# Squares of q and k taken by ACT ahead of the mixers, with two buffers, and two pairs' scalings on POOL

## The chip, the cores and the metric

The kernel runs on one core of one Trainium2 chip. The metric is the device time of one execution in microseconds (us); the time of a kernel is the median of its runs.

## The reference

Four batches of twelve heads (448 tokens, 64 columns) go through attention with normalised queries and keys, and its output through two mixers of tokens and channels.

```python
def rmsnorm(x, g):
    return x / np.sqrt(np.mean(x * x, axis=-1, keepdims=True) + 1e-06) * g
scores = (rmsnorm(q, g_q) @ rmsnorm(k, g_k).T) / 8          # per head
attn = exp(scores - max) / (sum + 1e-9); out = attn @ v
x = out of all heads, as [4, 448, 768]
u = x + (x.T @ U @ V).T;  x = u + relu(u @ w_ch1) @ w_ch2    # first mixer, 3072 wide
u = x + (relu(x.T @ w_tok1) @ w_tok2).T
x = u + relu(u @ w_ch1') @ w_ch2'                            # second mixer, 1536 wide
```

The change touches `mean(x * x)` and the scaling of q and k by its root.

## The kernel before

All arithmetic is in 32 bits; products are made of parts (high and low) of 32-bit operands. Heads are taken in pairs: 24 pairs, numbered 0 to 23 in the order in which they are loaded (`turn`). Tokens lie on 112 partitions, four rows each.

The program has a lone stage, in which only the attention of the first two batches runs (pairs 0 to 11); a seam, in which the first mixer's weights begin to come in and the rank mix of these batches is made (`rank_mix`, x.T @ U @ V); a mixed stage, in which the first mixer of the first two batches runs with the attention of the last two among it (pairs 12 to 23); and then the mixers that are left. The generator `attention` (L505) prepares pairs ahead of the heads that it weighs, so pairs 12 to 16 are partly prepared within the lone stage.

One pair takes these steps. `fetch_heads` (L352) loads q, k and v from SP's queue; q and k share five buffers. `load_pair` (L364) squares q and k (L373, tile sq, one buffer), sums the squares per token on DVE (L374, tile ms), takes 1/sqrt by Ln and Exp on ACT (L378, L379, tile rs) and one Newton step in four small operations (L381 to L384, tile nt), and scales q and k (L392, tiles qn and kn). `split` (L143) then cuts v into a high part on ACT and a low part on POOL (tile vs). The squares and the scalings are on DVE for pairs 0, 2 and 3 and on POOL for all others; the small operations are on DVE for pair 0 and on POOL else. `turn_pair` (L404) transposes qn and kn on PE (tt), takes the high part on ACT (L417, L421) and the low part on DVE (both, one buffer for q and one for k), and copies them by DMA into qs and ks (L434, L433; L438 for pair 0), three buffers each. `softmax` (L442): two score products per quarter of a head on PE (sc, three PSUM buffers), their maximum on DVE (L451, nm), the exponential on ACT (L453, p), and the normalisation on POOL (L460). `weigh` (L463): transposition of p on PE (pt), copies into ph and pl, and the product with v.

Each engine takes its instructions in the order of its queue and waits at the head of it. The code's order is not the queues' order: a scheduler, which runs when the program is built, orders each engine's instructions by durations that it assumes, except where `keep_in_program_order` is set (the loads of the first weights). A changed instruction in the lone stage so moves others far behind it. A pool's tile that is used again makes its writer wait for the readers of the tile before.

Of the kernel before, what the change touches and what calls it, by code (L numbers as in the profile page):

```python
# [9 lines left out]
F32 = mybir.dt.float32  # L10
# [3 lines left out]
AF = mybir.ActivationFunctionType  # L14
# [10 lines left out]
def attention_then_two_mixers(  # L25
# [30 lines left out]
    nc = tc.nc  # L56
# [3 lines left out]
    CP, NC4 = 112, 4  # L60
    NP = H // 2
# [36 lines left out]
        return x.rearrange("r (p c) -> r c p", c=NC4)  # L98

    pools = {"late": False, "split_u": nc.gpsimd}  # L100
    AT = dict(qr=5, kr=5, vr=3, qn=1, vs=2, p=8, ph=3, pl=3, sq=1)

    def open_pools(stack, side):
        for nm, bufs, space in side:
            pools[nm] = stack.enter_context(tc.tile_pool(
                name=nm, bufs=bufs, **({"space": PSUM} if space else {}), reuse_waits="tile"))
# [36 lines left out]
    def split(w, hi, lo):  # L143
        nc.scalar.activation(hi, w, AF.Copy)  # L144
        nc.gpsimd.tensor_sub(lo, w, f(hi))  # L145
# [206 lines left out]
    def fetch_heads(b, hp, names):  # L352

        h0 = 2 * hp
        res = []
        for nm in names:
            t = pools["at"].tile([CP, 2, NC4, D], F32, tag="vr" if nm == "v" else "qkr", bufs=AT[nm + "r"],
                        name=f"{nm}r")
            nc.sync.dma_start(t, dict(q=q, k=k, v=v)[nm][b, h0:h0 + 2].rearrange(
                "h (p c) d -> p h c d", c=NC4))  # L360
            res.append(t)
        return res

    def load_pair(b, hp, whole, turn, qk):  # L364
        first = turn == 0
        mul = nc.vector.tensor_mul if turn in (0, 2, 3) else nc.gpsimd.tensor_mul
        qr, kr, vr = qk + fetch_heads(b, hp, "v")

        ms = pools["at"].tile([CP, 2, 8], F32, tag="ms", name="ms")
        for i, t in enumerate((qr, kr)):  # L370
            sq = pools["at"].tile([CP, 2 * NC4, D], F32, tag="sq", bufs=AT["sq"], name="sq")
            tt = t.rearrange("p h c d -> p (h c) d")
            mul(sq, tt, tt)  # L373
            nc.vector.reduce_sum(ms[:, i], sq, axis=AX.X)  # L374
        small = nc.vector if first else nc.gpsimd
        small.tensor_scalar(ms, ms, 1.0 / D, 1e-6, op0=ALU.mult, op1=ALU.add)
        rs = pools["at"].tile([CP, 2, 8], F32, tag="rs", name="rs")
        nc.scalar.activation(rs, ms, AF.Ln)  # L378
        nc.scalar.activation(rs, rs, AF.Exp, scale=-0.5)  # L379
        nt = pools["at"].tile([CP, 2, 8], F32, tag="nt", name="nt")  # L380
        small.tensor_mul(nt, rs, rs)  # L381
        small.tensor_mul(nt, nt, ms)
        small.tensor_scalar(nt, nt, -0.5, 1.5, op0=ALU.mult, op1=ALU.add)
        small.tensor_mul(rs, rs, nt)  # L384

        def scale(i, shape):
            return rs[:, i].rearrange("p (h c) -> p h c", h=2).unsqueeze(3).to_broadcast(shape)

        qn, kn = [], []
        for i, (nm, t, n) in enumerate((("qn", qr, qn), ("kn", kr, kn))):  # L390
            n.append(pools["at"].tile([CP, NC4, 2, D], F32, tag=nm, bufs=AT["qn"], name=nm))
            mul(  # L392
                n[0].rearrange("p c h d -> p h c d"), t, scale(i, [CP, 2, NC4, D]))
        qn, kn = qn[0], kn[0]

        vs = pools["at"].tile([CP, 2, NC4, 2, D], F32R, tag="vs", bufs=AT["vs"], name="vs")
        js = [j for j in range(2) if j not in whole]
        if js:
            js = slice(js[0], js[-1] + 1)
            split(vr[:, js], vs[:, js, :, 0], vs[:, js, :, 1])  # L400
        flat = vr.rearrange("p h c d -> p (h c d)")
        return qn, kn, [flat[:, j * NC4 * D:] if j in whole else vs[:, j] for j in range(2)]
# [39 lines left out]
    def softmax(pr, qs, ks, kt):  # L442
        for c in range(NC4):
# [7 lines left out]
            nc.vector.tensor_reduce(nm, sc, axis=AX.X, op=ALU.max, negate=True)  # L451
            p = pools["pp"].tile([CP, S], F32, tag="p", bufs=AT["p"], name="p")
            nc.scalar.activation(p, sc, AF.Exp, bias=nm, accum_out=sm[:, c % 2:c % 2 + 1])  # L453
# [9 lines left out]
    def weigh(pr, vj, j, dst, whole):  # L463
# [3 lines left out]
        def product(kc, ph, pl):  # L467
            if whole:
                mm(pv, vj[:, kc * D:kc * D + P], ph, kc == 0, kc == NC4 - 1)
                return  # L470
            vk = vj[:, kc].rearrange("p t d -> p (t d)")
            mm(pv, vk, ph, kc == 0, False)
            mm(pv, vk, pl, False, kc == NC4 - 1)

        last = None
        for kc in range(NC4):
# [6 lines left out]
            if last:  # L483
                product(*last)
            ph = pools["pp"].tile([CP, S], F32 if whole else F32R, tag="ph", bufs=AT["ph"],
                                  name="ph")
# [551 lines left out]
    with ExitStack() as stack:  # L1038
# [24 lines left out]
        w1s = [w1_chunk("a", wa1, j) for j in range(G)]  # L1063
        pools["late"] = False
        inner.close()
        AT.update(p=8, ph=3, pl=3)
        open_pools(stack, (("pp", 1, 0), ("g", 2 * G + 1, 0), ("p", 2, 1), ("v", 1, 1),
                           ("s", 2, 1), ("t", 1, 1), ("m", 2, 1)))
        pools["new_xs"] = lambda: pools["g"].tile([P, 2, S], F32R, tag="g", name="xs")
# [97 lines left out]
```

## Time and profile before

| | |
|---|---|
| median of three runs | 1530.44 us (1529.71 to 1535.4) |
| profiled execution | 1532.7 us, of which its span 1530.9 us |
| PE busy | 1440.5 us, 94% |
| DVE busy | 1170.5 us, 76% |
| POOL busy | 921.8 us, 60% |
| ACT busy | 742.7 us, 49% |

The page's shares are means over stages. Of its 40 slices of 38 us the first five are the lone stage; PE is busy 4, 8, 8, 9 and 9 tenths there, POOL 5, 8, 9, 9 and 8, and the granted clock of PE is at nine tenths or more in all of them; the sixth slice, the seam, has the lowest clock, 7 tenths. A busy PE isn't a PE at its peak, since a matmul's latency counts as busy.

### The profile page before, as it was taken

To read this page: it belongs to the slowest core of one execution; us is meant where nothing else is said; L and a number is where in the kernel's file an instruction comes from. 1 tells how busy PE (TensorE), PEld (TensorE's weight loads), DVE (VectorE), ACT (ScalarE), POOL (GpSimd) and SP (SyncE) were. 2 spreads that over 40 slices of the span, in tenths; PEclk is the share of its full clock that TensorE was granted. 3 is DMA by queue.
4 is the path that set the end of the run, shared out by engine and by line. 5 is a ranking of instruction groups with operands and counts; after the bars stand their busy time and mean duration, and the time that the engine had idled before them with its cause. 6 is when DMAs were issued, how large, how long until landed. Compare 5 with 4: busy or idle time off the path is not lost.

```text
span 1530.9 us, 22094 instructions
## 1 busy us (share of the span) xinstructions
PE 1440.5 (94%) x7396; PEld 1271.6 (83%) x7396; DVE 1170.5 (76%) x1793; ACT 742.7 (49%) x1508; POOL 921.8 (60%) x955
## 2 busy tenths in 40 slices
PE   4889978999999999999999999998999999999998
PEld 3667656888899889988888998897999998988997
DVE  7888777887877778666757766477888888578876
ACT  4777655656665665444535343335343431334421
POOL 5899857877876655455645454037777755206841
PEclk9999979999999999999999999999999999999999
DMA  6666545867766664765637664354545453424343
GB/s 171 159 163 162 145 162 183 250 193 218 253 220 203 184 208 171 258 227 175 214 128 240 227 231 143 116 194 134 177 127 183 127 186 129 134 85 127 119 122 103
DMA packets 144385, 266.06 MB, mean 174 GB/s; under 512 B 12832, under 2 KB 104448, under 8 KB 144160
## 3 DMA queue, kind: packets, MB, share of 16 engines
q1 hardware_dynamic: 143952, 264.65, 55.5%
q8 instruction: 59, 0.97, 0.3%
q14 instruction: 54, 0.44, 0.1%
q10 hardware_dynamic: 320, 0.00, 0.0%
HBM read 149.72 MB, written 79.10 MB: 149 GB/s over the span
## 4 chain that ended last, share of the span: by engine, by line
PE 63%; DVE 11%; POOL 8%; DMA 7%; ACT 5%; issue 4%; SPq 1%; ACTq 0%; POOLq 0%; DVEq 0%
PE ps_x L79 26%; PE ps_g L79 12%; PE ps_p L79 10%; PE pv L79 3%; PE sc L79 3%; PE pt L479 2%; POOL w_bits L134 2%; PE ps_u L79 2%; POOL w L145 2%; PE ps_t L79 2%; DMA qs<-both 2%; DVE w_bits L126 1%; POOL p L460 1%; DMA w_raw<-in_moe_w_ch_dram 1%; DMA c_a<-w_bits 1%
## 5 line engine op out<-in xcount | busy, mean ns | idle before, releaser
L79 PE MATMUL ps_x<-gs,w 128*128 128x448 f32 x1440 | 323.9, 371 | 9.6 <-DVE xT L668 5.3
L79 PE MATMUL ps_g<-u,w 128*128 128x448 f32 x1440 | 313.1, 370 | 4.3 <-DMA w<-h_a 1.8
L79 PEld LDWEIGHTS ps_x<-gs,w 128*128 128x128 f32 x1440 | 266.7, 189 | 35.4 <-DVE xT L668 8.4
L79 PEld LDWEIGHTS ps_g<-u,w 128*128 128x128 f32 x1440 | 269.4, 189 | 28.8 <-DVE u L565 2.1
L79 PE MATMUL ps_x<-gs,w_b 128*128 128x448 f32 x1026 | 228.8, 369 | 7.1 <-DVE xT L833 2.4
L79 PEld LDWEIGHTS ps_x<-gs,w_b 128*128 128x128 f32 x1026 | 192.9, 189 | 25.9 <-DVE xT L833 3.8
L134 POOL TENSOR_TENSOR w_bits<-w_bits,w_round 128x768 uint32<-128x768 uint32 (+3 forms) x80 | 144.9, 1812 | 109.3 <-DVE w_bits L131 59.5
L145 POOL TENSOR_TENSOR w<-w_bits,w 128x768 fp32r<-128x768 f32 (+3 forms) x82 | 145.4, 1780 | 73.1 <-ACT w L144 69.3
L668 DVE TENSOR_TENSOR xT<-ps_x,xT 128x448 f32<-128x448 f32 x216 | 132.2, 617 | 36.5 <-PE ps_x L79 33.7
L145 POOL TENSOR_TENSOR w_b<-w_f,w_b 128x384 fp32r<-128x384 f32 x104 | 118.3, 1152 | 59.1 <-ACT w_b L144 58.9
L295 POOL TENSOR_TENSOR w_f<-w_f 128x384 f32<-128x384 f32 x26 | 36.2, 1391 | 179.8 <-DMA w_f<-c_b 75.0
L460 POOL TENSOR_SCALAR p<-p,sm 112x448 f32<-112x448 f32 x192 | 133.1, 706 | 17.5 <-DVE sm L457 10.9
L453 ACT ACTIVATE p<-sc,nm 112x448 f32<-112x448 f32 x192 | 121.3, 635 | 45.8 <-DVE nm L451 40.3
L79 PE MATMUL sc<-ks,qs 128*112 128x448 f32 x384 | 120.9, 407 | 15.9 <-ACT p L453 11.3
L451 DVE TENSOR_REDUCE nm<-sc 112x1 f32<-112x448 f32 x192 | 116.2, 614 | 17.6 <-PE sc L79 16.8
L479 PEld LDWEIGHTS pt<-ident,p 112*112 112x112 f32 x768 | 89.8, 134 | 33.2 <-issue 10.4
L126 DVE TENSOR_SCALAR w_bits<-w_bits 128x768 f32<-128x768 f32 (+3 forms) x80 | 71.9, 898 | 56.6 <-ACT w_bits L125 56.5
L479 PE MATMUL pt<-ident,p 112*112 112x112 f32 x768 | 111.9, 261 | 2.5 <-DVE pl L494 0.8
L130 ACT ACTIVATE w_round<-w_raw 128x768 uint32<-128x768 uint32 (+3 forms) x80 | 69.8, 873 | 77.6 <-POOL w_bits L134 69.9
L490 ACT ACTIVATE ph<-pt 112x448 fp32r<-112x448 f32 (+1 forms) x168 | 88.2, 544 | 26.2 <-PE pt L479 25.5
L637 ACT ACTIVATE gs<-ps_g 128x448 fp32r<-128x448 f32 x88 | 47.3, 541 | 108.8 <-PE ps_g L79 107.9
L125 ACT ACTIVATE w_bits<-w_raw 128x768 f32<-128x768 f32 (+3 forms) x80 | 69.8, 874 | 61.7 <-POOL w L145 33.1
(141 smaller groups left out, 2766.2 us busy)
## 6 DMA issues: line engine op xcount, KB each, us to landing
w_raw<-in_moe_w_ch_dram SPq DMA_DIRECT2D x72, 768.0 KB, 5.1
w_b<-h_a SPq DMA_DIRECT2D x65, 384.0 KB, 4.3
h_a<-w SPq DMA_DIRECT2D x56, 384.0 KB, 3.1
ks<-both SPq DMA_DIRECT2D x92, 224.0 KB, 3.8
c_a<-w_bits SPq DMA_DIRECT2D x40, 384.0 KB, 4.7
w_f<-c_a SPq DMA_DIRECT2D x40, 384.0 KB, 3.2
h_b<-w SPq DMA_DIRECT2D x32, 384.0 KB, 2.6
w_b<-h_b SPq DMA_DIRECT2D x29, 384.0 KB, 3.8
```

Source lines behind the costliest of these rows:

```text
L79: nc.tensor.matmul(o, lhsT=l, rhs=r, start=start, stop=stop)
L125: nc.scalar.activation(f(w), f(high), AF.Abs)
L126: nc.vector.tensor_scalar_max(f(w), f(w), TINY)
L130: nc.scalar.activation(r, low, AF.Copy, scale=2.0 ** -29)
L134: nc.gpsimd.tensor_tensor(w, w, r, op=ALU.add)
L145: nc.gpsimd.tensor_sub(lo, w, f(hi))
L451: nc.vector.tensor_reduce(nm, sc, axis=AX.X, op=ALU.max, negate=True)
L453: nc.scalar.activation(p, sc, AF.Exp, bias=nm, accum_out=sm[:, c % 2:c % 2 + 1])
L460: nc.gpsimd.tensor_scalar(x, x, sm[:, i:i + 1], 1.0, op0=ALU.mult, op1=ALU.mult)
L479: nc.tensor.transpose(pt[:, c * CP:(c + 1) * CP], pr[c][:, kc * CP:(kc + 1) * CP], ident[:CP, :CP],)
L490: nc.scalar.activation(ph, pt, AF.Copy)
L668: nc.vector.tensor_add(xT[:, dc], px, xT[:, dc])
```

## The change

Pair 0's q and both q and k of pairs 1 to 11 are squared by ACT (`AF.Square`); pair 0's k stays on DVE; from pair 12 on the squares stay on POOL. The scalings of pairs 2 and 3 go from DVE to POOL. The squares get two buffers; ms and nt get one instead of two; pl has two instead of three in the mixed stage.

```diff
--- before.py
+++ after.py
@@ -98,7 +98,7 @@
         return x.rearrange("r (p c) -> r c p", c=NC4)
 
     pools = {"late": False, "split_u": nc.gpsimd}
-    AT = dict(qr=5, kr=5, vr=3, qn=1, vs=2, p=8, ph=3, pl=3, sq=1)
+    AT = dict(qr=5, kr=5, vr=3, qn=1, vs=2, p=8, ph=3, pl=3, sq=2)
 
     def open_pools(stack, side):
         for nm, bufs, space in side:
@@ -363,21 +363,26 @@
 
     def load_pair(b, hp, whole, turn, qk):
         first = turn == 0
-        mul = nc.vector.tensor_mul if turn in (0, 2, 3) else nc.gpsimd.tensor_mul
+        mul = nc.vector.tensor_mul if first else nc.gpsimd.tensor_mul
         qr, kr, vr = qk + fetch_heads(b, hp, "v")
 
-        ms = pools["at"].tile([CP, 2, 8], F32, tag="ms", name="ms")
+        ms = pools["at"].tile([CP, 2, 8], F32, tag="ms", bufs=1, name="ms")
         for i, t in enumerate((qr, kr)):
             sq = pools["at"].tile([CP, 2 * NC4, D], F32, tag="sq", bufs=AT["sq"], name="sq")
             tt = t.rearrange("p h c d -> p (h c) d")
-            mul(sq, tt, tt)
+            if turn >= NP * 2:
+                nc.gpsimd.tensor_mul(sq, tt, tt)
+            elif first and i:
+                nc.vector.tensor_mul(sq, tt, tt)
+            else:
+                nc.scalar.activation(sq, tt, AF.Square)
             nc.vector.reduce_sum(ms[:, i], sq, axis=AX.X)
         small = nc.vector if first else nc.gpsimd
         small.tensor_scalar(ms, ms, 1.0 / D, 1e-6, op0=ALU.mult, op1=ALU.add)
         rs = pools["at"].tile([CP, 2, 8], F32, tag="rs", name="rs")
         nc.scalar.activation(rs, ms, AF.Ln)
         nc.scalar.activation(rs, rs, AF.Exp, scale=-0.5)
-        nt = pools["at"].tile([CP, 2, 8], F32, tag="nt", name="nt")
+        nt = pools["at"].tile([CP, 2, 8], F32, tag="nt", bufs=1, name="nt")
         small.tensor_mul(nt, rs, rs)
         small.tensor_mul(nt, nt, ms)
         small.tensor_scalar(nt, nt, -0.5, 1.5, op0=ALU.mult, op1=ALU.add)
@@ -1063,7 +1068,7 @@
         w1s = [w1_chunk("a", wa1, j) for j in range(G)]
         pools["late"] = False
         inner.close()
-        AT.update(p=8, ph=3, pl=3)
+        AT.update(p=8, ph=3, pl=2)
         open_pools(stack, (("pp", 1, 0), ("g", 2 * G + 1, 0), ("p", 2, 1), ("v", 1, 1),
                            ("s", 2, 1), ("t", 1, 1), ("m", 2, 1)))
         pools["new_xs"] = lambda: pools["g"].tile([P, 2, S], F32R, tag="g", name="xs")
```

Lines behind the edit have numbers higher by five (L378 to L383, L392 to L397, L453 to L458). Three places, one of them on two engines, show how the queues' orders move. Numbers behind a tile's name count the tiles in the order of the code; qr_113, kr_115 and vr_121 are loads of pair 0, qr_117, kr_119 and vr_182 of pair 1, qr_178 and kr_180 of pair 2.

The head of the program on ACT: rs_131 is pair 0's root, both_151 and both_159 are its turned q and k. Before:

```order
L378 ACTIVATE rs_131<-ms_123 112x16
L379 ACTIVATE rs_131<-rs_131 112x16
L144 ACTIVATE vs_143<-vr_121 112x4x64
L144 ACTIVATE vs_204<-vr_182 112x4x64
L417 ACTIVATE both_151<-tt_146,gg_78 128x448
L421 ACTIVATE both_159<-tt_154 128x448
L378 ACTIVATE rs_192<-ms_184 112x16
L379 ACTIVATE rs_192<-rs_192 112x16
```

Now, from the second square on:

```order
L378 ACTIVATE sq_185<-qr_117 112x512
L144 ACTIVATE vs_143<-vr_121 112x4x64
L378 ACTIVATE sq_188<-kr_119 112x512
L383 ACTIVATE rs_131<-ms_123 112x16
L144 ACTIVATE vs_204<-vr_182 112x4x64
L384 ACTIVATE rs_131<-rs_131 112x16
L378 ACTIVATE sq_280<-qr_178 112x512
L383 ACTIVATE rs_192<-ms_184 112x16
L384 ACTIVATE rs_192<-rs_192 112x16
L422 ACTIVATE both_151<-tt_146,gg_78 128x448
L378 ACTIVATE sq_283<-kr_180 112x512
L426 ACTIVATE both_159<-tt_154 128x448
```

The two operations of rs_131 stood first; now two squares and the two splits of v stand ahead of or between them, and the square of kr_180 stands ahead of both_159.

POOL in the lone stage, while pair 0 and pair 1 are normalised (L460, L465) and pairs 3 and 4 are prepared (rs_502 and nt_505 are pair 3's, sq_710 and sq_713 pair 4's). Before:

```order
L381 TENSOR_TENSOR nt_505<-rs_502 112x16
L456 TENSOR_SCALAR sm_337<-sm_337 112x2
L373 TENSOR_TENSOR sq_710<-qr_488 112x512
L382 TENSOR_TENSOR nt_505<-nt_505,ms_494 112x16
L456 TENSOR_SCALAR sm_374<-sm_374 112x2
L460 TENSOR_SCALAR p_343<-p_343,sm_337 112x448
L460 TENSOR_SCALAR p_358<-p_358,sm_337 112x448
L383 TENSOR_SCALAR nt_505<-nt_505 112x16
L456 TENSOR_SCALAR sm_414<-sm_414 112x2
L373 TENSOR_TENSOR sq_713<-kr_490 112x512
L460 TENSOR_SCALAR p_380<-p_380,sm_374 112x448
L460 TENSOR_SCALAR p_397<-p_397,sm_374 112x448
```

Now:

```order
L465 TENSOR_SCALAR p_343<-p_343,sm_337 112x448
L465 TENSOR_SCALAR p_358<-p_358,sm_337 112x448
L386 TENSOR_TENSOR nt_505<-rs_502 112x16
L387 TENSOR_TENSOR nt_505<-nt_505,ms_494 112x16
L461 TENSOR_SCALAR sm_374<-sm_374 112x2
L388 TENSOR_SCALAR nt_505<-nt_505 112x16
L389 TENSOR_TENSOR rs_502<-rs_502,nt_505 112x16
L397 TENSOR_TENSOR qn_510<-qr_273,rs_502 112x2x4x64
L397 TENSOR_TENSOR kn_512<-kr_275,rs_502 112x2x4x64
L381 TENSOR_SCALAR ms_709<-ms_709 112x16
L465 TENSOR_SCALAR p_380<-p_380,sm_374 112x448
L465 TENSOR_SCALAR p_397<-p_397,sm_374 112x448
```

The squares of pair 4 are gone from between the normalisations; the scalings of pair 3 (qn_510, kn_512) have come, and the sums of pair 4 (ms_709) are taken up right behind them.

ACT at the same place, among the exponentials (p). Before:

```order
L453 ACTIVATE p_358,sm_337<-sc_353,nm_356 112x448
L417 ACTIVATE both_465<-tt_460,gg_78 128x448
L453 ACTIVATE p_380,sm_374<-sc_375,nm_378 112x448
L453 ACTIVATE p_397,sm_374<-sc_392,nm_395 112x448
L490 ACTIVATE ph_316<-pt_311 112x448
L453 ACTIVATE p_420,sm_414<-sc_415,nm_418 112x448
L421 ACTIVATE both_473<-tt_468 128x448
L453 ACTIVATE p_438,sm_414<-sc_433,nm_436 112x448
L490 ACTIVATE ph_351<-pt_345 112x448
L453 ACTIVATE p_523,sm_517<-sc_518,nm_521 112x448
```

Now:

```order
L458 ACTIVATE p_380,sm_374<-sc_375,nm_378 112x448
L383 ACTIVATE rs_502<-ms_494 112x16
L378 ACTIVATE sq_710<-qr_488 112x512
L384 ACTIVATE rs_502<-rs_502 112x16
L378 ACTIVATE sq_713<-kr_490 112x512
L458 ACTIVATE p_397,sm_374<-sc_392,nm_395 112x448
L458 ACTIVATE p_420,sm_414<-sc_415,nm_418 112x448
L378 ACTIVATE sq_925<-qr_703 112x512
L495 ACTIVATE ph_388<-pt_383 112x448
L495 ACTIVATE ph_410<-pt_403 112x448
L458 ACTIVATE p_438,sm_414<-sc_433,nm_436 112x448
```

Three squares of pairs 4 and 5 stand among the exponentials and the copies of the transposed p (ph).

ACT in the seam: xs are parts of the transposed x, u the mixed x, w_bits and w_round the first steps of a weight chunk. Before:

```order
L586 ACTIVATE xs<-ps_h 128x384
L558 ACTIVATE xs<-pt_x 112x384 x2
L564 ACTIVATE u<-xT 128x448
L558 ACTIVATE xs<-pt_x 112x384
L564 ACTIVATE u<-xT 128x448
L558 ACTIVATE xs<-pt_x 112x384
L125 ACTIVATE w_bits<-w_raw 128x768
L130 ACTIVATE w_round<-w_raw 128x768
L564 ACTIVATE u<-xT 128x448
L125 ACTIVATE w_bits<-w_raw 128x768
```

Now:

```order
L591 ACTIVATE xs<-ps_h 128x384
L563 ACTIVATE xs<-pt_x 112x384 x2
L569 ACTIVATE u<-xT 128x448
L125 ACTIVATE w_bits<-w_raw 128x768
L130 ACTIVATE w_round<-w_raw 128x768
L569 ACTIVATE u<-xT 128x448
L563 ACTIVATE xs<-pt_x 112x384 x2
L125 ACTIVATE w_bits<-w_raw 128x768
L569 ACTIVATE u<-xT 128x448
L144 ACTIVATE w<-w_bits 128x768
```

The second chunk's w_bits and w_round have moved ahead of the second u and of the last turned parts of x.

## Rows read from the trace of the kernel before

**Rows 1.** Stretches: us, busy of PE, PEld, DVE, ACT, POOL; clock, DMA, GB/s
```profile
22.00:60.00 38.00, 32.23 (x159) 23.54 (x160) 32.29 (x67) 26.51 (x74) 28.97 (x57) 0.91 0.70 176
60.00:100.00 40.00, 34.72 (x203) 25.68 (x201) 33.91 (x72) 29.15 (x82) 33.68 (x60) 1.00 0.66 159
100.00:130.00 30.00, 28.54 (x162) 20.72 (x161) 25.04 (x53) 23.74 (x67) 27.58 (x52) 1.00 0.61 150
130.00:196.00 66.00, 61.13 (x347) 43.64 (x345) 54.82 (x114) 46.63 (x127) 58.14 (x112) 1.00 0.64 159
196.00:245.00 49.00, 36.26 (x150) 28.56 (x150) 35.85 (x48) 27.42 (x50) 31.29 (x22) 0.79 0.45 154
245.00:560.00 315.00, 302.23 (x1638) 267.77 (x1639) 256.39 (x441) 196.41 (x410) 228.84 (x251) 0.99 0.71 219
```

**Rows 2.** Chain of work by line, 22 to 130 us, then 130 to 165
```profile
by line: PE sc L79 15.8%; PE pv L79 14.9%; DMA qs<-both 11.9%; PE pt L479 9.4%; DMA ks<-both 8.9%; issue 8.3%; ACT p L453 7.1%; SPq L433 5.3%; PE tt L410 3.8%; ACT ph L490 3.4%; DVE nm L451 2.2%; SPq L434 2.0%; ACT w L144 1.2%; ACT both L41
...
by line: POOL p L460 14.3%; issue 12.8%; DMA qs<-both 10.3%; DMA kr<-in_k_dram 8.8%; DVE nm L451 6.5%; POOL sq L373 6.0%; PE pv L79 4.5%; DVE both L418 3.7%; DVE ms L374 3.6%; DVE ph L488 3.3%; PE sc L79 3.1%; POOL qn L392 3.0%; POOL sm L45
```

**Rows 3.** Weight loads of PE waiting, 22 to 130: us, times, longest
```profile
PEld sc L79 <- ACT p L453: 10.1, 16, 1.7
```

**Rows 4.** Groups, 22 to 130: busy, mean ns of one, idle before it
```profile
L453 ACT ACTIVATE p<-sc,nm 112x448 f32<-112x448 f32 x64 | 40.4, 637 | 6.0 <-DVE nm L451 3.9 <-PE pt L479 2.0
...
L373 POOL TENSOR_TENSOR sq<-qr 112x512 f32<-112x512 f32 x8 | 8.6, 1080 | 2.2 <-DMA qr<-in_q_dram 1.7
...
L373 POOL TENSOR_TENSOR sq<-kr 112x512 f32<-112x512 f32 x8 | 8.3, 1039 | 0.5 <-DMA kr<-in_k_dram 0.3
...
L392 POOL TENSOR_TENSOR qn<-qr,rs 112x512 f32<-112x512 f32 x6 | 6.3, 1043 | 0.4
```

**Rows 5.** The same view, whole execution, one shape on ACT
```profile
L144 ACT ACTIVATE vs<-vr 112x512 fp32r<-112x512 f32 x12 | 7.5, 627 | 2.7 <-PE pv L79 2.7
```

**Rows 6.** The head in order of time: start, us, instruction, idle before it
```profile
0.72 1.28 ACT L82 ACT_TABLE_LOAD   x1 [0.72 <-PEq L1151]
...
7.93 0.17 DVE L381 TENSOR_TENSOR nt<-rs 112x16 f32<-112x16 f32 x1
...
8.41 0.42 ACT L144 ACTIVATE vs<-vr 112x256 fp32r<-112x256 f32 x1 [1.58 <-DMA vr<-in_v_dram]
...
9.69 1.48 DVE L392 TENSOR_TENSOR qn<-qr,rs 112x512 f32<-112x512 f32 x1
...
9.80 0.42 ACT L144 ACTIVATE vs<-vr 112x256 fp32r<-112x256 f32 x1 [0.97 <-DMA vr<-in_v_dram]
...
11.20 0.31 SPq L359 DMA_DIRECT2D kr<-in_k_dram  x1
...
13.41 0.54 ACT L421 ACTIVATE both<-tt 128x448 fp32r<-128x448 f32 x1 [0.44 <-PE tt L410]
...
14.91 2.48 SPq L438 DMA_DIRECT2D ks<-both  x4
...
18.00 1.43 PE L79 MATMUL sc<-ks,qs 128*112 128x448 f32 x3
...
20.60 0.69 DVE L392 TENSOR_TENSOR qn<-qr,rs 112x512 f32<-112x512 f32 x1 [2.09 <-POOL rs L384]
...
21.82 0.62 DVE L451 TENSOR_REDUCE nm<-sc 112x1 f32<-112x448 f32 x1
```

**Rows 7.** DMA issues up to 14 us: KB each, us to landing
```profile
kr<-in_k_dram SPq DMA_DIRECT2D x3, 224.0 KB, 3.4
```

**Rows 8.** The start of the rank mix in order of time
```profile
206.34 11.43 SPq L116 DMA_DIRECT2D w_raw<-in_moe_w_ch_dram  x3
...
213.09 0.91 ACT L125 ACTIVATE w_bits<-w_raw 128x768 f32<-128x768 f32 x1
```

**Rows 9.** DMA issues, whole execution: KB each, us to landing
```profile
w_raw<-in_moe_w_ch_dram SPq DMA_DIRECT2D x72, 768.0 KB, 5.1
```

**Rows 10.** Writes of pl, 245 to 570 us: ns min, median, max
```profile
L494 DVE TENSOR_TENSOR pl<-pt,ph x80: 593/615/626, 264.2 to 567.0; 112x448 fp32r<-112x448 f32 x80
```

## The prediction

> **What bounds the kernel now.** I read the stretches first [rows 1], since the shares of a whole span mix stages with different limits. From 245 to 560 us PE is busy 302.2 of 315 us, so what ACT and POOL do there matters only where PE is idle; behind that stretch the queues' orders are the same with and without the change. From 196 to 245 us, the seam with the first weights, PE has 36.3 of 49 us at a mean granted clock of 0.79. The attention alone ("lone stage") runs up to 196 us, and there no engine has the whole time: between 22 and 130 us PE is busy 32.2 + 34.7 + 28.5 = 95.5 of 108 us (12.5 idle), DVE 91.2, POOL 90.2, ACT 79.4. The edited squares lie almost all in this part: sixteen on POOL between 22 and 130 us [rows 4]. After 130 us POOL squares only for pair 12 and later (pair 11's second square is the last ahead of it), and those stay with POOL.
>
> Second, the chain of work that ended last [rows 2]. Between 22 and 130 us it runs through PE (score, transposition and value products, 43.9% together with tt), through the copies of the turned q and k (qs and ks, 20.8%) and through ACT's exponentials (7.1%). No POOL line is among those named there. Between 130 and 165 us POOL does carry it: its normalisations have 14.3%, its squares 6.0%. The reader is to see that the busy engine and the engine on the chain are not the same before 130 us, and that where POOL's squares are on the chain, they are the ones that the change leaves alone.
>
> Third, what PE waits for between 22 and 130 us [rows 3]: 10.1 us in 16 waits for ACT to have read a score tile. ACT is the idlest of the four by busy time and yet the one that PE waits for, because its queue is in order.
>
> **The change part by part.** I work against the profiled execution, 1532.7 us with a span of 1530.9, and carry the differences over to the median of the three runs, 1530.4.
>
> *The head.* Before, the first correction of pair 0 (nt) starts at 7.93 and the scaled q at 9.69 [rows 6]. Now Ln of pair 0 stands on ACT behind the split of v (vr_121) and behind the square of kr_119, and the split of the next v stands between Ln and Exp. Those splits start at 8.41 and 9.80, each the moment its load landed [rows 6]; nothing moves these loads. So: split 8.41 to 8.83, square (0.63) to 9.46, Ln to 9.67, next split 9.80 to 10.22, Exp to 10.43, against nt at 7.93 before: 2.5 us later. DVE has one more reduction of this shape ahead of rs, so rs is some 3 us late; the scaled q, which took 1.48 us beside POOL's work, should now take the 0.69 of the same operation at 20.60 [rows 6], and starts near 12.7. The sixth q or k load (kr_180) waits for that q's buffer: before it was issued at 11.20, as the scaling at 9.69 ended; now near 13.4 and lands 3.4 us later [rows 7], at 16.8. On ACT the square of kr_180 now stands ahead of pair 0's turned k (both_159), which before began at 13.41 [rows 6]; it is held until 17.4. From the issue of the ks copies to the first scores it was 14.91 to 18.00, 3.1 us; so now 18.0 to 21.1 [rows 6]. That is 3.1 us late, but before, the first maximum did not follow the scores: it waited until 21.82, because DVE stood in front of the scaling of pair 2 (20.60, idle 2.09 for POOL) [rows 6]. That scaling is on POOL now, and the maximum can follow its second score products by about 1.9 us, near 23.0. The head costs **+1.2**; the bounds are -0.5 (if loads and copies land earlier than I shift them) and +3.1 (the scores' whole delay).
>
> *DVE loses five squares and four scalings.* Those before 21.8 us are in the head. Behind it lie one square and the two scalings of pair 3, 3 x 0.69 = 2.0 us [rows 6], on an engine that is busy 32.3 of 38 us [rows 1]. PE is idle 5.8 us in that stretch, partly for copies that no DVE square holds up. I take half: **-1.0**, bounds 0 and -2.0.
>
> *POOL loses sixteen squares* between 22 and 130 us, 8.6 + 8.3 = 16.9 us, and gets two scalings at 1.04 [rows 4], net 14.8 us of 90.2. This is the change's main effect and is off the chain [rows 2]. It can only help through what queues behind a square: the normalisations that PE's transpositions need. The ceiling is PE's idle time of 6.7 us from 60 to 130 us [rows 1] and a little before, 7. Since no POOL line is on that chain I take less than half: **-3.0**, bounds 0 and -7.
>
> *ACT gets the squares*: 23 of them (pair 0's q, both of pairs 1 to 11). The nearest row is the split of v in the same shape, 112x512, 0.627 us [rows 5]; the other end is the exponential, 0.637 for 448 columns [rows 4], 0.73 for 512. I take 0.63: 14.5 us. Six of them fall before 22 us; the other 17, 10.7 us, raise ACT's busy time up to 130 us from 79.4 to 90.1 us, 13%. If what PE waits for ACT grows in proportion, 10.1 x 0.13 = **+1.3**; bounds 0 (the squares fall into ACT's idle time, 28.6 us) and +5 (half of those 10.1 us again).
>
> The Trainium skill's page "ScalarE: Activation LUTs", section "Rules for kernel authors", speaks against this move: multiplications belong on VectorE, not on ScalarE. The rows show 0.63 for ACT's pass over this shape and 0.69 for DVE's multiplication of it [rows 5, 6]; by the page's rule the 17 squares would lie on DVE as 11.7 us beside its 91.2, which would fill 95% of the 108 us. Here the measurement decides against the rule: per square ACT is not slower.
>
> *Seam.* ACT now reaches the second weight chunk (w_bits, w_round) ahead of u and of the last turned x. Its load goes out at 206.34 [rows 8] and takes about 5.1 us [rows 9], so it lands near 211.5; before, ACT took it at 213.09 [rows 8]. Now u and x come up to two instructions of 0.91 later, but the chunk is ready 1.5 us sooner. **+0.5**, bounds 0 and +2.
>
> *What costs nothing.* pl with two buffers: of 80 writes [rows 10] I set each against the reads of PE, and only one came while two earlier ones were unread; it would wait for one read, on DVE, with PE busy. ms and nt with one buffer: the next pair's sums now wait until nt has been multiplied by ms; the order puts the sums behind that multiplication, so I price it at 0; if a sum does stand in front of it, the maxima queue behind it on DVE (in ACT's +5). sq with two buffers lets POOL square q and k in a row in the mixed stage, beside a full PE: 0. The orders of the mixed stage differ up to about 560 us; its 12.8 us of PE idle time [rows 1] can move by some 3 us either way, with no sign.
>
> Sum: +1.2 - 1.0 - 3.0 + 1.3 + 0.5 = -1.0: 1531.7 against the profiled 1532.7, and **1529.5** from the median of 1530.4.
>
> **The rivals.** *Relief pays in full.* POOL's shorter queue brings normalisations and scaled q and k forward, and the copies of qs and ks, a fifth of the chain, start earlier. Then the two gains reach their ends, -2 - 7, ACT's cost and the seam are 0 and the head +0.5: 1522; with 3 us from the mixed stage 1519. For it: POOL is busy 27.6 of 30 us at 100 to 130 us. Against: POOL is not on the chain there. *ACT's queue is blocked*, slower than before. A square stands at the head of ACT's queue until its load has landed; on POOL one such wait of 1.7 us is on the rows [rows 4], where only POOL paid. On ACT the exponentials and the turned q and k queue behind it, and PE waits for these. Pairs 3 to 11 have 17 squares behind 22 us; if half of them wait 1 us each, that is +8.5, and with the head at +3.1 and the other gains halved about +10: 1540. It decides from about one wait of 1 us in every pair on. *The change doesn't do what it says*: if Square needed another function table, each would bring table loads among the exponentials; the built program has one table load, as before. 23 squares with two loads each, at the 1.28 us of the one load [rows 6], would be +59: 1589.
>
> **How the numbers follow.** Forecast (within 8 us) 0.62, relief in full 0.24, ACT blocked 0.13, tables 0.01. A measurement of this kernel can tell about 0.5%, 7.7 us, from no change. The range is 1519 to 1539: about half of the relief case lies below it and two thirds of the blocked case above it, 0.2 together. Faster by over 0.5% 0.24, within 0.62, slower 0.14.
>
> **What the changed profile would show.** Right: squares of about 0.63 us on ACT; the first maximum near 23 us; POOL busy about 75 us from 22 to 130 us; PE's idle time there 10 to 13 us; the seam (196 to 245 us before) as long as before within 2 us. The POOL term is wrong if PE's idle time between 60 and 130 us falls under 3 us, the ACT term if squares on ACT wait for loads over 5 us in all or PE's waits for ACT exceed 14 us. I would be wrong altogether if the mixed stage, from 245 us on, changed its length by more than 4 us.

## The result, and the profile after

| | before | after |
|---|---|---|
| median of the runs, us | 1530.4 | 1550.4 |
| ratio to before, 95% interval | | 1.0138, 1.0118 to 1.0158 |
| profiled execution: time and its span, us | 1532.7 and 1530.9 | 1548.3 and 1546.1 |
| first maximum of pairs 0, 6, 9, 11, 12 (start, us) | 21.8, 100.9, 141.0, 167.6, 246.0 | 22.8, 103.8, 149.9, 177.4, 255.8 |
| first product for u (ps_g), start, us | 213.2 | 222.6 |
| from there to the 727th such product, us | 464.1 | 469.1 |
| from there to the end, us | 853.6 | 854.4 |

The kernel is 1.4% slower; the forecast was 1529.5 with a range up to 1539. One of five runs of the kernel before took 7658.4 us, for which the record has no reason, and the ratio leaves it out. The products for u (tile ps_g) are those of u with the first weights of a mixer, as in `u @ w_ch1`; each execution has 1584. The last three lines of the table cut the execution at points of the same work: lone stage and seam, mixed stage (all the attention that is left lies within these 727 products; it ends at 631.4 us before and at 628.3 after), and the rest. The lone stage gives 9.4 us, the mixed stage 5.0, the rest 0.8. A second profile of each kernel (e7 and e8 below) gives 8.1, 9.5 and 5.0. On the mean of both, 8.8 us come from the lone stage, 7.2 from the mixed stage and 2.9 from the rest, 18.9 together.

The stretches of the kernel after that answer to [rows 1], same columns:

```profile
22.00:60.00 38.00, 31.50 (x159) 22.31 (x159) 31.29 (x65) 30.57 (x84) 24.62 (x56) 0.98 0.80 194
60.00:100.00 40.00, 35.83 (x201) 26.05 (x199) 32.84 (x71) 30.71 (x82) 28.67 (x60) 0.98 0.66 160
100.00:130.00 30.00, 26.97 (x146) 19.76 (x144) 23.69 (x49) 23.61 (x63) 23.56 (x46) 0.94 0.57 138
130.00:196.00 66.00, 58.64 (x328) 44.33 (x328) 52.47 (x108) 46.94 (x129) 52.35 (x99) 0.95 0.60 140
196.00:245.00 49.00, 37.30 (x167) 27.75 (x165) 32.41 (x48) 25.82 (x47) 27.57 (x23) 0.86 0.44 148
245.00:560.00 315.00, 298.60 (x1603) 262.89 (x1603) 257.40 (x433) 198.16 (x410) 231.46 (x252) 0.98 0.69 212
```

Up to 100 us little is lost. From 100 to 196 us PE is busy 85.6 us against 89.7 in [rows 1], and at a granted clock of 0.94 and 0.95 where it had 1.00. POOL has become emptier, as meant (76.9 of 108 us from 22 to 130), and so has PE.

What ACT and PE's weight loads wait for in the lone stage, 60 to 205 us, in the kernel after (us in total, times, longest):

```profile
PEld sc L79 <- ACT p L458: 18.6, 18, 2.7
...
ACT both L422 <- DMA qs<-both: 12.5, 6, 3.3
```

and in the kernel before:

```profile
PEld sc L79 <- ACT p L453: 9.4, 17, 1.7
...
ACT both L417 <- DMA qs<-both: 5.3, 3, 2.4
```

L422 (L417 before) is ACT's high part of the turned q. There is one buffer for it, so it waits until the copies of the previous pair's q (qs) have landed. Before, it waited three times there; now six times, and PE's wait for ACT's exponentials has doubled. No square is in these rows. One such place, that of pair 10, in the kernel after, ACT's and PE's rows in order of time (start, us, instruction, idle before it):

```profile
140.94 0.54 ACT L507 ACTIVATE tmp<-pv 64x448 f32<-64x448 f32 x1
...
141.06 0.59 SPq L439 DMA_DIRECT2D qs<-both  x1
...
141.50 0.54 ACT L495 ACTIVATE ph<-pt 112x448 f32<-112x448 f32 x1
...
145.35 0.63 ACT L422 ACTIVATE both<-tt,gg 128x448 fp32r<-128x448 f32 x1 [3.31 <-DMA qs<-both]
...
145.88 0.63 ACT L458 ACTIVATE p<-sc,nm 112x448 f32<-112x448 f32 x1
...
146.49 0.63 ACT L458 ACTIVATE p<-sc,nm 112x448 f32<-112x448 f32 x1
...
146.66 0.77 PE L79 MATMUL sc<-ks,qs 128*112 128x448 f32 x2 [1.96 <-ACT p L458]
...
147.10 0.64 ACT L458 ACTIVATE p<-sc,nm 112x448 f32<-112x448 f32 x1
```

The last copy of q is issued at 141.06 and ACT is let go at 145.35. Three exponentials, whose scores and maxima are ready, stand behind L422 in the queue. PE has filled its score tiles and sits idle for 1.96 us until the first exponential has read one. At 100 us (pair 7) the q waits no longer than before, 1.7 us, but three steps of a weight (w and w_round, up to 101.3 us) now stand behind it and ahead of all three exponentials; in the kernel before one of the three stood ahead of these steps. And the stall costs more than itself, as the stretches around it show:

```profile
143.00:147.00 4.00, 2.04 (x13) 1.29 (x12) 1.26 (x3) 1.65 (x4) 3.56 (x6) 1.00 0.52 147
147.10:150.50 3.40, 3.40 (x16) 2.87 (x13) 2.92 (x7) 2.76 (x9) 1.84 (x5) 0.50 0.36 77
150.60:154.00 3.40, 3.40 (x27) 3.03 (x27) 3.40 (x9) 2.72 (x7) 0.74 (x1) 1.00 0.74 170
```

Behind the idle time the granted clock stands at 0.50, the lower of its two levels (1.2 GHz), for 3.4 us, in which PE is busy all the time and issues 16 products instead of 27. The same follows PE's waits for ACT that begin at 100, 172 and 294 us, 2.0 to 2.2 us each.

The kernel before has the turned q of pair 11 behind the three exponentials:

```profile
148.45 0.54 ACT L502 ACTIVATE tmp<-pv 64x448 f32<-64x448 f32 x1
...
149.01 0.54 ACT L490 ACTIVATE ph<-pt 112x448 f32<-112x448 f32 x1
...
149.65 0.63 ACT L453 ACTIVATE p<-sc,nm 112x448 f32<-112x448 f32 x1
...
150.28 0.62 ACT L453 ACTIVATE p<-sc,nm 112x448 f32<-112x448 f32 x1
...
150.88 0.63 ACT L453 ACTIVATE p<-sc,nm 112x448 f32<-112x448 f32 x1
...
152.48 0.64 ACT L417 ACTIVATE both<-tt,gg 128x448 fp32r<-128x448 f32 x1 [0.44 <-DMA kr<-in_k_dram]
```

Pair 9's stands there so too, and pair 10's behind one of its three; neither waits. But the order isn't new everywhere: in the kernel before too the turned q of pairs 5 to 8 stands ahead of exponentials, as here for pair 6, and waits 1.0 to 1.7 us:

```profile
82.18 0.64 ACT L417 ACTIVATE both<-tt,gg 128x448 fp32r<-128x448 f32 x1 [1.25 <-DMA qs<-both]
...
82.72 0.63 ACT L453 ACTIVATE p<-sc,nm 112x448 f32<-112x448 f32 x1
...
83.33 0.63 ACT L453 ACTIVATE p<-sc,nm 112x448 f32<-112x448 f32 x1
...
83.93 0.64 ACT L453 ACTIVATE p<-sc,nm 112x448 f32<-112x448 f32 x1
```

In the kernel after it stands ahead of the three for pairs 6, 8 to 10, 12 and 13. Pairs 9 and 10 wait 2.4 and 3.3 us where they had not waited, and pairs 6 and 8 wait longer in the same place (2.5 us against 1.2, 2.0 against 1.0); why longer isn't shown.

**Theory A**: the squares on ACT made the scheduler put the turned q of more pairs ahead of three exponentials, where it waits for copies, and this order, not the squares' time, is what costs in the lone stage. **Rivals**: the single buffers of ms and nt (B), the squares' own time on ACT (C), the pl buffer (D). **Theory E**, formed later, for the mixed stage: any new order costs there.

### The profile page after: what moved, and what is told of

Read it like the earlier page. It is cut to its first block, busy times and chain, and to the rows that moved or that the text cites. A ratio compares the mean times of both kernels' runs of the same rounds, so it can differ in the third digit from the quotient of the medians.

```text
span 1546.1 us, 22112 instructions
## 1 busy us (share of the span) xinstructions
PE 1449.2 (94%) x7396; PEld 1275.3 (82%) x7396; DVE 1163.8 (75%) x1784; ACT 757.2 (49%) x1531; POOL 909.6 (59%) x941
## 4 chain that ended last, share of the span: by engine, by line
PE 46%; DVE 9%; POOL 9%; DMA 5%; issue 4%; ACT 3%; SPq 0%; POOLq 0%; DVEq 0%; ACTq 0%
PE ps_x L79 21%; PE ps_g L79 9%; PE ps_p L79 8%; POOL w L145 2%; POOL w_bits L134 2%; PE ps_t L79 2%; PE ps_u L79 2%; DVE w_bits L126 1%; ACT w_bits L125 1%; DVE w_bits L131 1%; POOL w_b L145 1%; DMA w_f<-c_a 1%; DMA c_a<-w_bits 1%; ACT w L144 1%; DVE w_bits L127 1%
## 5 line engine op out<-in xcount | busy, mean ns | idle before, releaser
L79 PE MATMUL sc<-ks,qs 128*112 128x448 f32 x384 | 124.1, 416 | 28.3 <-ACT p L458 24.0
L465 POOL TENSOR_SCALAR p<-p,sm 112x448 f32<-112x448 f32 x192 | 132.1, 700 | 23.2 <-DVE sm L462 16.7
L458 ACT ACTIVATE p<-sc,nm 112x448 f32<-112x448 f32 x192 | 121.0, 634 | 46.1 <-DVE nm L456 32.3
L456 DVE TENSOR_REDUCE nm<-sc 112x1 f32<-112x448 f32 x192 | 116.3, 612 | 18.4 <-PE sc L79 17.7
L126 DVE TENSOR_SCALAR w_bits<-w_bits 128x768 f32<-128x768 f32 (+3 forms) x80 | 76.2, 953 | 61.8 <-ACT w_bits L125 61.6
L484 PE MATMUL pt<-ident,p 112*112 112x112 f32 x768 | 108.7, 260 | 1.9 <-POOL p L465 1.1
L79 PEld LDWEIGHTS sc<-ks,qs 128*112 128x112 f32 x384 | 62.4, 187 | 47.6 <-ACT p L458 36.7
L495 ACT ACTIVATE ph<-pt 112x448 fp32r<-112x448 f32 (+1 forms) x168 | 88.8, 543 | 23.7 <-PE pt L484 22.7
```

Source lines behind the costliest of these rows:

```text
L79: nc.tensor.matmul(o, lhsT=l, rhs=r, start=start, stop=stop)
L126: nc.vector.tensor_scalar_max(f(w), f(w), TINY)
L465: nc.gpsimd.tensor_scalar(x, x, sm[:, i:i + 1], 1.0, op0=ALU.mult, op1=ALU.mult)
L484: nc.tensor.transpose(pt[:, c * CP:(c + 1) * CP], pr[c][:, kc * CP:(kc + 1) * CP], ident[:CP, :CP],)
L495: nc.scalar.activation(ph, pt, AF.Copy)
```

## Experiments

All in one table, read from the trace of each: first product for u; ACT's waits for copies of q and PE's weight loads waiting for ACT's exponentials, both 60 to 205 us; the mixed stage from the first to the 727th product for u.

| | time, us | ratio to before, interval | first u | q waits | p waits | mixed |
|---|---|---|---|---|---|---|
| before | 1530.4 | | 213.2 | 5.3 | 9.4 | 464.1 |
| e7, before again | 1529.2 | 1.0003 (0.998 to 1.0027) | 213.2 | 1.8 | 9.5 | 463.5 |
| after | 1550.4 | 1.0138 (1.0118 to 1.0158) | 222.6 | 12.5 | 18.6 | 469.1 |
| e8, after again | 1550.2 | 1.0145 (1.0107 to 1.0182) | 221.3 | 12.6 | 19.9 | 473.0 |
| e1, squares on ACT alone | 1548.5 | 1.0128 (1.0105 to 1.0151) | 221.0 | 13.5 | 18.1 | 472.3 |
| e2, squares back | 1538.0 | 1.0058 (1.0039 to 1.0078) | 212.7 | 0 | 5.5 | 472.1 |
| e3, after, two turned q | 1531.1 | 1.0000 (0.9981 to 1.0019) | 204.8 | 0 | 10.4 | 467.9 |
| e4, pl alone | 1537.8 | 1.0048 (1.0025 to 1.0072) | 214.2 | 3.3 | 9.9 | 469.8 |
| e5, q held behind | 1548.5 | 1.0133 (1.0109 to 1.0158) | 214.4 | 3.3 | 10.1 | 483.3 |
| e6, before, two turned q | 1518.2 | 0.992 (0.9874 to 0.9966) | 204.0 | 0 | 5.4 | 457.9 |
| e9, ms and nt alone | 1534.1 | 1.0028 (1.0008 to 1.0048) | 214.1 | 5.6 | 12.5 | 467.2 |
| e10, six p alone | 1536.3 | 1.0048 (1.0025 to 1.0071) | 213.3 | 5.8 | 11.8 | 471.2 |
| e11, e6 with scalings | 1518.3 | 0.992 (0.9897 to 0.9944) | 206.8 | 0 | 5.9 | 459.3 |

**e1: the squares on ACT alone.** The kernel before with, in `load_pair`:

```
-            mul(sq, tt, tt)
+            if turn >= NP * 2:
+                nc.gpsimd.tensor_mul(sq, tt, tt)
+            elif first and i:
+                nc.vector.tensor_mul(sq, tt, tt)
+            else:
+                nc.scalar.activation(sq, tt, AF.Square)
```

> The kernel before with one part of the change: the squares up to pair 11 on ACT (pair 0's k on DVE, pairs 12 and later on POOL), with one sq buffer, two for ms and nt, three for pl, and the scalings of pairs 2 and 3 on DVE as before. Theory A (the squares put the turned q at the head of ACT's queue, where it waits for the copies of the pair before, and the exponentials queue behind it): this part alone gives most of the loss: the first product for u starts at 219 to 224 us (213.2 before, 222.6 after), ACT's waits for the copies of q from 60 to 205 us are over 9 us, the time 1540 to 1552 us. Theory B (the single buffers of ms and nt are the cause): the first product for u within 3 us of 213, the time 1526 to 1536 us.

Waits from 60 to 205 us in its trace:

```profile
PEld sc L79 <- ACT p L458: 18.1, 20, 2.9
ACT both L422 <- DMA qs<-both: 13.5, 8, 3.3
```

These are the rows of the kernel after. The squares alone make the loss of the lone stage, and nearly the whole loss of time. B falls.

**e2: the squares back.** The kernel after, its squares as before:

```
-            if turn >= NP * 2:
...
-                nc.scalar.activation(sq, tt, AF.Square)
+            (nc.vector if turn in (0, 2, 3) else nc.gpsimd).tensor_mul(sq, tt, tt)
```

> The kernel after with one part undone: the squares on DVE for pairs 0, 2 and 3 and on POOL else, as before; two sq buffers, one for ms and nt, two for pl and the scalings of pairs 2 and 3 on POOL stay. Theory A: the loss goes: the first product for u starts at 210 to 217 us, ACT's waits for the copies of q from 60 to 205 us are under 6 us, the time 1525 to 1536 us. Theory B (single buffers): it stays, 219 us or later, 1542 to 1552 us.

The lone stage is as before and the waits for copies of q are gone, so of the change's parts it is the squares that bring the loss there. But the time stays 7.6 us above before: the mixed stage takes 472.1 us. Theory A says nothing of that.

**e3: a second buffer for the turned q.** The kernel after with:

```
-                                    bufs=1, name="both")
+                                    bufs=2 if scale else 1, name="both")
...
-        AT.update(p=8, ph=3, pl=2)
+        AT.update(p=6, ph=3, pl=2)
```

> The kernel after with a second buffer for the turned q (both), so that ACT's high part of the next q needn't wait for the copies of the one before; the room is taken from the exponentials' tiles of the mixed stage (p with six buffers for eight there; the lone stage keeps its twelve). Theory A: ACT's waits for the copies of q from 60 to 205 us fall from 14.0 us to under 4, the first product for u starts at 211 to 217 us. Rival C (the squares' own time on ACT is what the exponentials lose): the waits go elsewhere, the first product for u stays at 220 to 225 us. The whole time also holds what six p buffers cost in the mixed stage, so the lone stage is read from the trace.

(The 14.0 us named there count from 23 us on; from 60 us they are 12.5.) Waits from 60 to 205 us in its trace:

```profile
PEld sc L79 <- ACT p L458: 10.4, 18, 1.4
...
ACT both L426 <- DMA ks<-both: 4.6, 5, 2.3
```

The turned q doesn't wait any more, the turned k does a little, and the first product for u starts at 204.8, earlier than the 211 to 217 expected and 8.4 us ahead of the kernel before. The squares are still on ACT, so C is refuted as the cause of the loss.

**e5: the turned q held behind.** The kernel after; `exps` collects the exponentials in the order of the code, `turns` counts the pairs:

```
-                nc.scalar.activation(hi, tt, AF.Copy, scale=scale)
+                turns.append(0)
+                with tc.issue_after(exps[-8 + 0]) if 3 < len(turns) <= 12 else ExitStack():
+                    nc.scalar.activation(hi, tt, AF.Copy, scale=scale)
...
-            nc.scalar.activation(p, sc, AF.Exp, bias=nm, accum_out=sm[:, c % 2:c % 2 + 1])
+            exps.append(nc.scalar.activation(p, sc, AF.Exp, bias=nm, accum_out=sm[:, c % 2:c % 2 + 1]).ins)
```

> The kernel after with one order held: from the fourth pair to the twelfth, ACT's high part of the turned q (L422) is issued behind the first exponential of the first head of the pair ahead; the built order then puts it behind three exponentials where the kernel after had it ahead of them. All work, squares on ACT too, and all buffers stay. Theory A (order): the exponentials no longer queue behind the wait for the copies, the first product for u starts at 212 to 218 us (222.6 after), the time 1535 to 1545 us. Rival C (the squares' own time on ACT): the same work is still there, the first product for u stays at 220 to 225 us and the time at 1547 to 1553.

ACT's rows at the place shown above (pair 10), now:

```profile
136.30 0.63 ACT L462 ACTIVATE p<-sc,nm 112x448 f32<-112x448 f32 x1
...
136.92 0.62 ACT L462 ACTIVATE p<-sc,nm 112x448 f32<-112x448 f32 x1
...
137.53 0.63 ACT L462 ACTIVATE p<-sc,nm 112x448 f32<-112x448 f32 x1
...
139.58 0.63 ACT L424 ACTIVATE both<-tt,gg 128x448 fp32r<-128x448 f32 x1 [1.33 <-DMA ks<-both]
...
140.12 0.97 ACT L499 ACTIVATE ph<-pt 112x448 fp32r<-112x448 f32 x2
```

There is still a wait, shorter and by the profile for a copy of k, but the three exponentials stand ahead of it, and behind it come two copies of the transposed p. All squares are on ACT, all buffers are those of the kernel after, and the first product for u starts at 214.4, 8.2 us earlier than in the kernel after. Theory A holds for the lone stage, C falls. The time that it expected was missed all the same: 1548.5, because the mixed stage took 483.3 us. What the holding gained in one stage the new order lost in the next.

**e4: pl alone.** The kernel before with `AT.update(p=8, ph=3, pl=2)` in place of `pl=3`; the queues' orders agree with before up to about 196 us.

> The kernel before with one part of the change: pl with two buffers in place of three in the mixed stage. The queues' orders are the same as before up to about 196 us. It tells what the mixed stage's order alone can move. Theory A (the loss is made in the lone stage, and the mixed stage's order moves some 3 us either way): the first product for u at 213 within 1 us, the time 1527 to 1535 us. Rival D (the buffer of pl costs in the mixed stage): 1535 us or more.

PE's weight loads waiting for pl, 245 to 610 us, before and then in e4:

```profile
PEld pv L79 <- DVE pl L494: 1.8, 4, 0.7
```

```profile
PEld pv L79 <- DVE pl L494: 5.2, 7, 1.8
```

The missing buffer is waited for, 3.4 us more, and the mixed stage is 5.7 us longer. The time, 1537.8, lies where D had it and not within A's 1527 to 1535: rival D has its share of the loss. It isn't needed for it: e1 has three pl buffers and the mixed stage takes 472.3 us there.

**e6: two buffers for the turned q, squares as before.** The edit of e3 on the kernel before (`p=6, ph=3, pl=3`).

> The kernel before with a second buffer for the turned q and six p buffers for eight in the mixed stage (squares as before, on DVE and POOL). With the kernel before, the squares on ACT alone and the kernel after with two such buffers (first product for u 213.2, 221.0, 204.8 us) it makes the four corners of squares by buffers. If the squares on ACT help once the wait is gone (my POOL term was right behind a wait), this one's first product for u is later than 204.8: 207 to 211 us. If only the buffer helps and the squares do nothing, 203 to 206. If it is under 203, the squares cost even without the wait.

204.0: once the wait is gone, the whole change (204.8 in e3) is worth nothing in the lone stage, neither a gain nor a loss that I can tell. The corners don't single out the squares, since e3 has the scalings of pairs 2 and 3 on POOL and e6 hasn't; e11 below has. With 1518.2 us it beats both kernels.

**e7 and e8: the two kernels again.** No edit; second profiles.

> The kernel before, unchanged, for a second profile of it. It tells how far two executions of one program differ in the stretches that I compare: the first product for u within 1.5 us of 213.2; and whether products in the last mixers (1050 to 1250 us) run at 249 in 50 us, as in the first profile, or at 243 to 244, as in the profiles of the squares alone and of two turned q, both at a granted clock of 1.00. Theory A says nothing on the latter; if it comes and goes in one program, it is no effect of the change.

> The kernel after, unchanged, for a second profile of it: the first product for u within 1.5 us of 222.6, ACT's waits for the copies of q from 60 to 205 us at 12 to 17 us (15.3 in the first profile); the pace of the products from 1400 to 1500 us, 486 in the first profile against 495 before, may be either.

(The 15.3 us named there are the 12.5 of the table and one wait of 2.8 that the profile puts down to "issue".) From 1050 to 1250 us the products of e7 run at 248 to 249 in 50 us, as in the first profile; from 1400 to 1500 us e8 has 487. The lone stage repeats within 1.3 us in either program, so the differences of 8 us above are not chance. The mixed stage repeats within 0.6 us before and within 3.9 after. The total of ACT's waits before varies (5.3 and 1.8) without PE's changing.

**e9: ms and nt alone.** The kernel before with `bufs=1` for ms and nt.

> The kernel before with one part of the change: one buffer in place of two for ms and nt; nothing else is added, moved or made longer, but the built order differs from the first pairs on. Theory B is already weak (with the squares back and these single buffers the lone stage was as before). Theory E (any new order of the mixed stage costs, since before's happens to be a good one: 464.1 and 463.5 us from the first product for u to the 727th in its two profiles, against 469 to 483 in the six kernels changed so far that kept eight p buffers): the stage takes 468 us or more, the first product for u starts within 3 us of 213.2, the time 1533 to 1545 us. Against it (the buffers cost nothing and order neither): the stage 462 to 466 us, the time 1527 to 1533.

(The six kernels named there are five, one of them in two profiles.) 467.2 lies between what the two theories said, and so does the time. A cost of this part is shown (1.0028, 1.0008 to 1.0048), theory E is not settled by it.

**e10: six p buffers alone.** The kernel before with `p=6` in place of `p=8` in the mixed stage, the control for e3, e6 and e11.

> The kernel before with six p buffers for eight in the mixed stage and no second buffer for the turned q: the control for the two kernels that have both. The lone stage has the order of the kernel before. If the second buffer for the turned q is what made that kernel faster (1518.2 us), this one is at 1529 to 1540 us, with the mixed stage at 463 us or more; if the six p buffers did it, its mixed stage takes about 458 us and its time 1522 to 1527.

Six buffers cost 5.9 us. Against this control the second buffer for the turned q is worth 1536.3 - 1518.2 = 18.1 us, 9.3 of them up to the first product for u and 13.3 in the mixed stage, with some given back behind it.

**e11: e6 with the scalings and squares of pairs 2 and 3 on POOL.** The edit of e6 and:

```
-        mul = nc.vector.tensor_mul if turn in (0, 2, 3) else nc.gpsimd.tensor_mul
+        mul = nc.vector.tensor_mul if first else nc.gpsimd.tensor_mul
```

> The kernel before with a second buffer for the turned q and six p buffers in the mixed stage, and with all squares and scalings of pairs 1 and later on POOL (pairs 2 and 3 too). With the squares and scalings of pairs 2 and 3 on DVE this was 1518.2 us, first product for u at 204.0. If the relief of DVE in the head is worth what I priced (1 us), the first product for u is at 202 to 204 us; the time 1512 to 1524 us, the mixed stage's order moving it by some 5 us either way.

First product for u 2.8 us later than in e6, time the same. The relief of DVE isn't worth 1 us here; that term was not borne out. e11 is also the nearer control for e3, which differs from it in the lone stage by the squares on ACT and the buffers of sq, ms and nt: 204.8 against 206.8 us. So with the wait gone the squares on ACT may gain some 2 us there; with one profile of each and 1.3 us between two profiles of one program that isn't shown.

**The mixed stage.** PE's busy time and clock over the same 727 products, in the kernels before and after, e1, e5 and e6, one row each (columns as in [rows 1]):

```profile
213.20:677.30 464.10, 442.65 (x2358) 392.20 (x2357) 369.38 (x608) 275.94 (x547) 312.76 (x316) 0.99 0.66 211
```

```profile
222.60:691.70 469.10, 445.42 (x2357) 391.99 (x2356) 371.91 (x609) 277.86 (x549) 316.01 (x316) 0.99 0.66 209
```

```profile
221.00:693.30 472.30, 445.97 (x2358) 394.51 (x2357) 374.55 (x608) 277.01 (x548) 313.85 (x316) 0.98 0.65 207
```

```profile
214.40:697.70 483.30, 453.43 (x2358) 398.60 (x2357) 366.88 (x608) 277.43 (x548) 313.64 (x316) 0.96 0.65 203
```

```profile
204.00:661.90 457.90, 442.02 (x2359) 390.53 (x2358) 362.77 (x609) 276.41 (x549) 317.15 (x316) 0.99 0.68 214
```

The number of products is the same. What differs is PE's idle time (length less busy: 21.5, 23.7, 26.3, 29.9, 15.9 us) and the time that the same products take (442.0 to 453.4 us, longest where the granted clock is 0.96). e1 has the work and the buffers of the kernel before in this stage, and only another order; it takes 8.2 us longer. All seven changed kernels with one buffer for the turned q, the kernel after among them, took 467 to 483 us, where both executions of before took 464. That is what theory E says, though all of them but e1 also have fewer buffers there. What made the lone stage longer isn't it: from the first to the 727th product the turned q waits for its copies 18.4 and 21.4 us in the two profiles before, 16.4 and 19.7 after. PE waits a little more for ACT's exponentials (6.0 and 6.6 us before, 8.6 and 8.1 after) and for pl (1.1 and 0.7, then 2.7 and 3.8). Some 1 us may be the slower pace of the last section, an estimate: 458 and 481 products of this stage start 204.5 to 210 ns behind the one ahead before, 762 and 724 after, and the two paces are 4 ns apart; but e1, with 527, takes as long. Which places of the order cost isn't found, and which of them the kernel after would share with e1 stays open.

## Why the prediction was wrong, point by point

**The step that failed is "ACT gets the squares".** I named ACT's in-order queue as the reason why PE waits for it, and then scaled PE's 10.1 us of waiting by ACT's added busy time, +1.3 with a bound of +5. The waiting here didn't follow the busy time: from 22 to 130 us ACT's went from 79.4 to 84.9 us, 7%, and PE's wait for its exponentials from 10.1 to 14.7, 46%. It followed which instruction stood at the head of the queue (e5). The term was +1.3; lone stage and seam lost 8.8 us on the mean of both profiles, about 1.4 of it in the head. The squares took the 0.63 us that I forecast, waited 1.9 us for loads between 22 and 130 us (my mark was 5), and did no harm of their own (e3, e5). What grew was the wait of the turned q, an instruction that the diff doesn't touch. Between the first maxima of pairs 6 and 11 the kernel after takes 73.6 us against 66.7, with only two squares of ACT in it (the last starts at 118.0). My rival "ACT's queue is blocked" had the engine and the victims right and the blocker wrong, and so a price of 10 us at 0.13. The mark that I set, PE's waits for ACT over 14 us from 22 to 130 us, was passed, 14.7.

**The order.** I compared orders only where I expected an effect, and priced order changes in the lone stage at nothing. The built order showed L422 ahead of three exponentials for pairs 9 and 10 too, where L417 had stood behind some of them, and the trace of before held a first price for such a place: three waits of L417 for the copies of q from 60 to 205 us, 1.2 to 2.4 us each.

**The head**: +1.2 forecast, +1.0 and +1.7 in the two pairs of profiles, the first maximum at 22.8 against "near 23.0". Right, and by the path that I named: the square of kr_180 starts at 16.8, the turned k behind it at 17.3 (17.4 forecast), the first scores at 20.8 (21.1).

**POOL's relief**, -3.0: POOL's busy time from 22 to 130 us came out as forecast, 76.9 us against some 75. The gain didn't show: PE's idle time there was 13.7 us, over the 10 to 13 forecast, and from 60 to 130 us 7.2, where it had been 6.7. Where no q waits, e3 against e11 (204.8 and 206.8 us) leaves room for a gain of some 2 us. So in the kernel after, the warning that no POOL line was on the chain [rows 2] was the better guide, and half of a ceiling was not; whether the wait hid a gain is open.

**DVE's relief**, -1.0: not seen; in e11 the same step comes with 2.8 us more. With it the whole change stands at 204.8 us against 204.0 where no q waits.

**Seam**, +0.5: pair 11's first maximum and pair 12's, on either side of it, are both 9.8 us late, so the seam is as long as before. Right, within the 2 us given.

**"What costs nothing"**: pl with two buffers cost 7.3 us on its own (0.25 to 0.72%). I had set each write against PE's reads in the order of before; in the order that was built, PE's weight loads wait 5.1 us for pl, against 1.8. ms and nt cost 3.7 us alone (0.08 to 0.48%), not 0.

**The mixed stage**, 3 us either way, "wrong altogether" over 4: it is 5.0 and 9.5 us longer. This is the second step that failed, with 7.2 of the 18.9 us; its cause stays open, but for a share that pl has (e4). A spread without a sign was the wrong model of it: each of the seven other orders that I ran with one buffer for the turned q was a longer one.

The 2.9 us behind the mixed stage had no term. (The sum itself is 1529.4, 1530.4 less 1.0, and not 1529.5.)

The Trainium skill's page "ScalarE: Activation LUTs", section "Rules for kernel authors", speaks for VectorE in multiplications, for its speed per element, with a figure for bf16. The result, slower, is on its side, but the runs don't bear out speed as the cause: a square took 0.63 us on ACT, a multiplication of that shape 0.69 us on DVE [rows 6], and with two buffers for the turned q the lone stage was no longer with the squares on ACT (204.8 us in e3) than on POOL (206.8 in e11). No run here has all these squares on VectorE.

## What to carry to other kernels

Before a step is moved to an in-order engine, list what on that engine waits for DMA with a single buffer, and see in the built order what now stands behind it; a wait already in the trace gives a first price, but here the waits grew too, from 2.4 us at most to 3.3. If such a wait exists, take it away first: here a second buffer gave 18 us, 12 of them left after the price of the two others it was paid with, where the whole change gave the lone stage nothing. And in a scheduled kernel price "another order" of a stage by what single small edits of it show (here 3 to 8 us, all losses), not as zero.

## What the hardware showed that I had not expected

At the granted clock of 1.00 the same products run at one of two paces. The stretch 1080 to 1160 us, PE busy throughout, in the kernel after and in its second profile (e8):

```profile
1080.00:1160.00 80.00, 80.00 (x397) 74.19 (x396) 71.51 (x80) 31.16 (x61) 62.38 (x56) 1.00 0.51 159
```

```profile
1080.00:1160.00 80.00, 80.00 (x389) 72.66 (x388) 70.13 (x77) 31.69 (x63) 61.48 (x56) 1.00 0.48 148
```

397 products against 389 in one program; from start to start the trace has 202.7 against 206.7 ns. In the first profile the slower pace comes later, from 1400 us:

```profile
1400.00:1480.00 80.00, 80.00 (x389) 72.67 (x388) 61.56 (x69) 34.81 (x64) 49.90 (x44) 1.00 0.45 140
```

Between these two stretches lies one with the granted clock at 0.50, at 1389 us, and from 1080 to 1300 us the pace had been the faster one. Such a fall isn't needed for a change of pace: in e8 it is back at 202.7 ns by 1360 us, and the clock stays at 1.00 from 1066 to 1547 us. A pace that is 2% slower for 300 us is 6 us, as much as several effects in the table, so the stages are compared by their own work. It comes and goes in one program, so it is not an effect of the change; its cause isn't in these rows. Part of the 2.9 us behind the mixed stage may be this.
